# Attention and gated long convolution in one kernel: q, k, v on 96 partitions, q transposed by DMA, o in 64x64 tiles, and a new time order

## The chip, the cores and the metric

The kernel runs on one core of one Trainium2 chip. The metric is the device time of one execution in microseconds (us), the median of several runs. The core's engines work side by side, each on its own list of instructions: TensorE (PE) multiplies matrices, VectorE (DVE), ScalarE (ACT) and GpSimd (POOL) work element by element, and SyncE (SP) issues DMAs. POOL and ACT issue DMAs as well. An engine that waits for a semaphore holds everything behind it on its own list.

## The reference: what is computed

The inputs are q, k, v as float32 arrays of 8 batches x 8 heads x 576 times x 64, g_norm (64), w_proj (512x1536), filter_fft (576x512) and w_out (512x512).

```
kv  = einsum('bhsd,bhse->bhde', k, v)              # per head, 64x64
out = einsum('bhsd,bhde->bhse', q, kv)             # linear attention
x   = out / sqrt(mean(out*out, -1) + 1e-6) * g_norm # then heads side by side: B, 576, 512
x1, x2, x3 = split(x @ w_proj, 3)
x2c = irfft(rfft(x2, axis=1) * rfft(filter_fft, axis=0), n=576)
result = (x1 * x2c * x3) @ w_out                   # B, 576, 512
```

The sum over time in kv doesn't depend on the order of the 576 times. Everything after it depends on that order only through the tables of the transform, the rows of the filter and the rows that the result is written to.

## The kernel before, in words

**Time order.** The kernel keeps the 576 times in an order of its own: three thirds of 192 times for a transform of radix 3, and within a third three blocks of 64 times that lie 3 apart. On 128 partitions a block of 64 is half a tile. The same order is built into the tables of sines and cosines (`tvi`, L120), into the filter's rows `fa` and `fc` (L139 to L148), and into the rows of the result (`o_rows`, L475).

**Loads.** All loads go through POOL's DMA queue and turn float32 into bfloat16 on the way. k and v of a batch come as four DMAs (`load_kv`, L67): the main part puts four times of a head on each of 128 partitions (runs of 1 KB in memory), and a tail of 64 times goes to `kt`, `vt`, whose upper half stays zero. q comes as two DMAs (`load_q`, L77) in the kernel's time order, runs of 768 B. There are two buffers of each, so batch b+2 is loaded during batch b into the buffers that batch b used.

**Attention of batch b+1** is done during batch b. `kv` (L215) makes the 64x64 products of the heads in 40 matmuls (L223) and ACT copies the result into the block diagonal `kvblk` (L234). `qtr` (L236) transposes q on TensorE in 36 small transposes into PSUM (L247), and ACT copies that to `qT` in two copies (L256, DVE in batch 0). `att_o(b, j)` (L258), for each of the four pairs of heads j, multiplies `qT` with `kvblk` in two matmuls (L265); ACT takes the square `sq` (L266) and the copy `osb` (L271). `att_r` (L273) sums the squares over a head with a matmul, and ACT makes `rstd` (L281). DVE multiplies (`att_x`, L289) and folds the thirds (`fold`, L291 to L307).

**Convolution of batch b.** `proj2` (L363) projects x to x2 in the frequency order's folded form; `fft(b, g)` (L388) transforms in three groups g = 1, 0, 2 and multiplies with the filter (L408, L409, L417), the adds that make Y being on POOL for group 1, and in batch 0 for group 0 too (L411). `proj13(b, dc)` (L419) makes a quarter of x1 and x3 in 16 matmuls (L428); ACT copies x1 (L432) and DVE multiplies to `g13` (L434). `inv` (L436) transforms back from Y (L454, L456), `outp` (L480) multiplies with w_out (L488, L492), ACT copies to `ot` (L496; three buffers), and SP writes the rows (L499, L501). The output of batch b-1 is made during batch b. In the last batch `last` (L521) ends with five pieces `out1` (L503), whose DMAs (L519) go out on SP and in part on POOL or ACT.

**PSUM** is four tiles `ps` that every product takes in turn (L54), so a matmul may have to wait until ACT or DVE has emptied a tile.

**Order.** The program text gives the order as priorities; a scheduler then places the instructions of each engine, with some held in program order by `keep_in_program_order`. The loop that sets the order in each batch is this:

```
for dc in range(NDC) if b else ():
    if dc < 3:
        add = fft(b, (1, 0, 2)[dc]) or add
    if nxt:
        att_o(b + 1, dc)
    proj13(b, dc)
    if dc == 2:
        add()
    if nxt:
        att_r(b + 1, dc)
        ...
```

Ahead of it in each batch stand `proj2(b)`, `kv(b + 1)`, `qtr(b + 1)` and the loads of batch b+2. `outp` stands after dc = 1 and after the loop, and `inv` ends the batch.

Of the kernel before, what the change touches and what calls it, by code (L numbers as in the profile page):

```python
# [15 lines left out]
P = 128  # L16
# [4 lines left out]
def kernel(  # L21
# [40 lines left out]
    NR = S // 64  # L62
    kvm = [[consts.tile([P, H, 4, D], BF16, name="%sm%d" % (n, i)) for n in "kv"] for i in range(2)]
    kvt = [[consts.tile([P, H, D], BF16, name="%st%d" % (n, i)) for n in "kv"] for i in range(2)]
    qb = [consts.tile([P, 4, NR * D], BF16, name="qb%d" % i) for i in range(2)]

    def load_kv(b, *parts):  # L67
        for h0, h1 in parts:
            for i, src in enumerate((k, v)):
                nc.gpsimd.dma_start(  # L70
                    out=kvm[b % 2][i][:, h0:h1].rearrange("p h c d -> p h (c d)"),
                    in_=bass.AP(tensor=src.tensor, offset=src.offset + (b * H + h0) * S * D,
                                ap=[[4 * D, P], [S * D, h1 - h0], [1, 4 * D]]))
                if h0 == 0:
                    nc.gpsimd.dma_start(out=kvt[b % 2][i][:TAIL], in_=src[b, :, 4 * P:S, :].transpose([1, 0, 2]))

    def load_q(b):  # L77
        for g in range(2):
            nc.gpsimd.dma_start(  # L79
                out=qb[b % 2][64 * g:64 * g + 64].rearrange("p h (m x) -> p (h m) x", m=3),  # L80
                in_=bass.AP(tensor=q.tensor, offset=q.offset + (b * H + 4 * g) * S * D,
                            ap=[[3 * D, 64], [SB * D, 12], [1, 3 * D]]))


    kvblk = [consts.tile([P, 4, P], BF16, name="kvblk%d" % i) for i in range(2)]
    for i in range(2):
        for t in kvt[i]:
            nc.vector.memset(t[TAIL:P], 0.0)
        nc.vector.memset(kvblk[i], 0.0)
# [15 lines left out]
    load_q(0)  # L105
# [14 lines left out]
    nc.gpsimd.iota(tvi, pattern=[[2 * SB, 2], [2, 3], [6, 64]], base=1, channel_multiplier=0)  # L120
# [17 lines left out]
    fidx = consts.tile([P, 3], I32)  # L138
    for a, r0, n, base in ((0, 0, 64, 0), (0, 64, 64, 1), (1, 0, 64, 2), (1, 64, 64, SB), (2, 0, 32, SB + 1)):  # L139
        nc.gpsimd.iota(fidx[r0:r0 + n, a:a + 1], pattern=[[0, 1]], base=S - 1 - base, channel_multiplier=-3)  # L140
    for r0, n, a, na, base, step in ((0, 64, 0, 2, 0, 2), (64, 64, 0, 2, 1, SB - 1), (0, 32, 2, 1, SB + 1, 1)):
        nc.gpsimd.dma_start(out=fa[r0:r0 + n, a:a + na], in_=bass.AP(
            tensor=moe_filter_fft.tensor, offset=moe_filter_fft.offset + base * DM,
            ap=[[3 * DM, n], [step * DM, na], [1, DM]]))
    for a in range(3):
        n = P if a < 2 else 32
        nc.gpsimd.indirect_dma_start(out=fc[:n, a], out_offset=None, in_=moe_filter_fft,
                                     in_offset=bass.IndirectOffsetOnAxis(ap=fidx[:n, a:a + 1], axis=0))  # L148

    load_q(1)  # L150
# [64 lines left out]
    def kv(b, j0=0, j1=NDC):  # L215
        (km, vm), (kt, vt) = kvm[b % 2], kvt[b % 2]
        kvp = ps_tile("ps_kv")
        for j in range(j0, j1):
            for c in range(NSC):
                for hp in range(2):  # L220
                    h = 2 * j + hp
                    kk, vv = (km[:, h, c], vm[:, h, c]) if c < 4 else (kt[:, h], vt[:, h])
                    mm = nc.tensor.matmul(kvp[64 * hp:64 * hp + 64, 0, j * D:(j + 1) * D], kk, vv,  # L223
                                          start=(c == 0), stop=(c == NSC - 1))
                    if b == 1:
                        tc.keep_in_program_order(mm)
        for h in range(2):
            r = slice(64 * h, 64 * h + 64)
            o_ = kvblk[b % 2][r, j0:j1, r]
# [5 lines left out]

    def qtr(b, jjs=(0, 1)):  # L236

        s = st.setdefault(b, {})
        if jjs[0] == 0:
            s['qTc'] = work.tile([P, NDC, NR, 64], BF16, name="qT", tag="qT")  # L240
            s['qT'] = s['qTc'].rearrange("p j c t -> p j (c t)")
        qT = s['qTc']
        for jj in jjs:
            tp = psp.tile([P, 2, 1024], BF16, name="ps_qT", tag="ps").rearrange("p a b -> p (a b)")
            for c in range(NR):
                for hp in range(2):
                    mm = nc.tensor.transpose(tp[64 * hp:64 * hp + 64, c * P:(c + 1) * P],  # L247
                                             qb[b % 2][:, 2 * jj + hp, c * D:(c + 1) * D], ident)
                    if b == 1:
                        tc.keep_in_program_order(mm)  # L250
            o_ = qT[:, 2 * jj:2 * jj + 2].rearrange("p g c t -> p c g t")
            i_ = tp[:, 0:NR * P].rearrange("p (c g t) -> p c g t", c=NR, g=2)
# [5 lines left out]
    def att_o(b, j):  # L258
        s = st[b]
        if j == 0:  # L260
# [291 lines left out]
    for b in range(B):  # L552
# [13 lines left out]
        elif nxt:  # L566
            kv(b + 1)
            qtr(b + 1)
# [75 lines left out]
```

## Time and profile before

| | |
|---|---|
| device time, median of 3 runs | 239.54 us (239.22 to 240.31) |
| span of the profiled execution | 238.0 us |
| PE busy | 213.9 us (90%) |
| DVE busy | 197.2 us (83%) |
| ACT busy | 156.0 us (66%) |
| POOL busy | 72.1 us (30%) |
| POOL's DMA queue | 40,256 packets, 17.70 MB |
| SP's and ACT's DMA queue | 5,122 packets, 8.92 MB |

The span runs from the first to the last recorded event of one profiled execution; some 1.5 us of the device time lie around it (239.54 less 238.0). The profile gives the busy time of each engine, the chain of work that ended last, followed back from the last instruction, groups of instructions by their source line, and a timeline of each engine in which a bracket tells how long the engine was idle before an instruction and what released it. A busy share is an average over the whole span and tells little of any one stage: the first 50 us are loads and tables, then six batches of nearly the same shape follow, then an end of its own.

### The profile page before, as it was taken

What the parts mean: (1) busy time and instruction counts of PE and PEld (TensorE: products, weight loads), DVE (VectorE), ACT (ScalarE), POOL (GpSimd) and SP (SyncE); (2) the same over time, 40 slices, a digit from 0 to 9 for tenths busy, and PEclk for the clock granted to TensorE, in tenths of its full rate; (3) what the DMA queues carried; (4) which work ended last, traced back from release to release, by engine and by line L of the source; (5) the groups of instructions that cost most, each with busy time, mean ns of one, the idle gap of its engine ahead of it and who ended that gap; (6) DMA issues with size and microseconds to landing.
All of it is one profiled execution on the core that took longest, in us unless ns stands there. A gap on an engine that the chain in (4) does not pass through costs nothing.

```text
span 238.0 us, 4900 instructions
## 1 busy us (share of the span) xinstructions
PE 213.9 (90%) x1960; PEld 128.5 (54%) x1960; DVE 197.2 (83%) x376; ACT 156.0 (66%) x237; POOL 72.1 (30%) x96
## 2 busy tenths in 40 slices
PE   4978897685999999999999999999999999999960
PEld 1434354363576657665667566656675666566420
DVE  7759574799989798979797989797979897999860
ACT  2754528971887689776977697769776977642520
POOL 7963971490280029000910091002100210021010
PEclk9999999999999999999999999999999999999997
DMA  6999999999099129914992399250033003400346
GB/s 63 163 190 230 227 192 197 191 192 108 3 155 198 45 77 158 203 38 126 121 193 74 91 118 188 83 135 0 4 88 88 3 0 91 132 0 3 94 122 181
DMA packets 45559, 27.17 MB, mean 114 GB/s; under 512 B 22274, under 2 KB 40706, under 8 KB 45538
## 3 DMA queue, kind: packets, MB, share of 16 engines
q0 software_dynamic: 40256, 17.70, 58.8%
q1 hardware_dynamic: 5122, 8.92, 13.9%
q8 instruction: 15, 0.25, 0.4%
q10 hardware_dynamic: 160, 0.26, 0.4%
q14 instruction: 6, 0.05, 0.1%
HBM read 33.69 MB, written 9.44 MB: 181 GB/s over the span
## 4 chain that ended last, share of the span: by engine, by line
PE 61%; ACT 15%; DVE 8%; DMA 8%; issue 3%; POOL 3%; POOLq 0%; DVEq 0%; ACTq 0%
PE ps_x L428 20%; PE ps_out L488 10%; ACT qT L256 6%; PE ps_x L378 6%; DMA fc<-in_moe_filter_fft_dram,fidx 5%; DMA km<-in_k_dram 3%; PE ps_x L384 2%; PE ps_x L369 2%; PE ps_o L265 2%; PE ps_r L280 2%; ACT kvblk L234 2%; PE ps_invo L454 2%; PE ps_inve L454 2%; PE ps_kv L223 2%; ACT osb L271 2%
## 5 line engine op out<-in xcount | busy, mean ns | idle before, releaser
L428 PE MATMUL ps_x<-x,wp 128*128 128x288 bf16 x512 | 68.0, 286 | 1.5 <-DVE FX L210 1.5
L428 PEld LDWEIGHTS <-wp 128*128 128x128 bf16 x512 | 49.8, 98 | 15.3 <-issue 2.6
L411 POOL TENSOR_TENSOR Y<-tpw 128x1024 bf16<-128x1024 f32 (+1 forms) x9 | 21.2, 2354 | 68.7 <-PE ps_x L428 43.2
L434 DVE TENSOR_TENSOR g<-ps_x,x 128x576 bf16<-128x576 f32 x32 | 24.1, 754 | 9.8 <-ACT x L432 9.7
L432 ACT CAST x<-ps_x 128x576 bf16<-128x576 f32 x32 | 20.7, 646 | 10.4 <-PE ps_x L428 10.4
L70 POOL DMA_DIRECT2D km<-in_k_dram x9 | 7.8, 871 | 64.4 <-PE ps_kv L223 64.4
L488 PE MATMUL ps_out<-wo,yg 128*128 128x512 bf16 x112 | 26.6, 379 | 0.0
L281 ACT ACTIVATE rstd<-ps_r,bias_eps 128x576 bf16<-128x576 f32 x32 | 23.3, 742 | 4.8 <-PE ps_r L280 4.8
L496 ACT COPY ot<-ps_out 128x1024 f32<-128x1024 f32 (+1 forms) x17 | 15.9, 937 | 13.8 <-PE ps_out L488 13.8
L266 ACT ACTIVATE sq<-ps_o 128x576 bf16<-128x576 f32 x32 | 20.7, 653 | 5.6 <-PE ps_o L265 5.6
L408 DVE TENSOR_TENSOR tpw<-ps_X,HH 128x1024 f32<-128x1024 f32 (+1 forms) x16 | 19.5, 1221 | 5.1 <-PE ps_X L406 4.4
L271 ACT ACTIVATE osb<-ps_o,g_col 128x576 bf16<-128x576 f32 x28 | 20.8, 742 | 0.0
L409 DVE TENSOR_TENSOR tpw<-ps_X,HH 128x1024 f32<-128x1024 f32 (+1 forms) x16 | 19.4, 1213 | 0.0
L458 ACT COPY os<-ps_invo 128x576 f32<-128x576 f32 x14 | 9.0, 640 | 12.9 <-PE ps_x L372 5.1
L488 PEld LDWEIGHTS <-yg 128*128 128x128 bf16 x112 | 10.8, 98 | 10.4
L265 PE MATMUL ps_o<-qT,kvblk 128*128 128x288 bf16 x64 | 12.8, 287 | 3.7 <-ACT kvblk L234 2.1
L378 PE MATMUL ps_x<-wp,ab 128*128 128x512 bf16 x64 | 15.5, 381 | 0.6 <-DVE ab L307 0.3
L256 ACT COPY qT<-ps_qT 128x1152 bf16<-128x1152 bf16 x14 | 15.1, 1122 | 0.1
L280 PE MATMUL ps_r<-sq,ind 128*128 128x288 bf16 x64 | 13.1, 286 | 1.6 <-ACT osb L271 0.8
L79 POOL DMA_DIRECT2D qb<-in_q_dram x16 | 12.5, 784 | 6.3 <-DMA wp<-in_moe_w_proj_dram 3.1
L535 PE MATMUL ps_w<-kvblk,ind 128*128 128x512 bf16 x33 | 11.1, 486 | 3.7 <-DVE ind L103 3.4
L374 ACT CAST x<-ps_x 128x1024 bf16<-128x1024 f32 x8 | 8.1, 1016 | 8.4 <-PE ps_x L372 8.4
(177 smaller groups left out, 414.8 us busy)
## 6 DMA issues: line engine op xcount, KB each, us to landing
out_dram<-ot SPq DMA_DIRECT2D x28, 256.0 KB, 3.3
qb<-in_q_dram POOLq DMA_DIRECT2D x16, 288.0 KB, 7.1
km<-in_k_dram POOLq DMA_DIRECT2D x7, 512.0 KB, 6.2
vm<-in_v_dram POOLq DMA_DIRECT2D x7, 512.0 KB, 8.4
wp<-in_moe_w_proj_dram POOLq DMA_DIRECT2D x3, 512.0 KB, 10.6
out_dram<-ot SPq DMA_DIRECT2D x10, 128.0 KB, 3.2
km<-in_k_dram POOLq DMA_DIRECT2D x2, 256.0 KB, 5.6
kt<-in_k_dram POOLq DMA_DIRECT2D x8, 64.0 KB, 5.7
```

The costliest lines, as they stand in the source:

```text
L256: nc.scalar.copy(out=o_, in_=i_)
L266: nc.scalar.activation(out=s['sq'][:, j].rearrange("p (a b) -> p a b", a=2), in_=op[:, :, 0:TH], func=AF.Square)
L271: nc.scalar.activation(out=o_, in_=op[:, :, 0:TH], func=AF.Copy, scale=g_col)
L281: nc.scalar.activation(out=s['rstd'][:, j].rearrange("p (a b) -> p a b", a=2), in_=r2[:, :, 0:TH], func=AF.Abs_reciprocal_sqrt, scale=1.0 ...
L378: nc.tensor.matmul(pp[:, h], ab[:, j, h * SB:h * SB + P], wp[:, j, DM:2 * DM], start=(j == 0), stop=(j == NDC - 1))
L408: nc.vector.tensor_mul(out=t_[:n, 0], in0=xp[:n], in1=HH[:n, g, 1:3])
L409: nc.vector.tensor_mul(out=t_[:n, 1], in0=xp[:n], in1=HH[:n, g, 0:2])
L411: nc.gpsimd.tensor_add(out=Y[:n, 2 * g:2 * g + 2], in0=t_[:n, :, 0], in1=t_[:n, :, 1])
L428: nc.tensor.matmul(pp[:, h, 0:TH], w_, x[:, j, h * TH:(h + 1) * TH], start=(j == 0), stop=(j == NDC - 1))
L432: nc.scalar.copy(out=x1, in_=pp[:, :, 0:TH])
L434: nc.vector.tensor_mul(out=st[b]['g13'][:, dc].rearrange("p (a b) -> p a b", a=2), in0=pp[:, :, 0:TH], in1=x1)
L488: nc.tensor.matmul(pp[:, cc], yg[:, dc, c * P:(c + 1) * P], wo[:, dc], start=(dc == 0), stop=(dc == NDC - 1))
```

## The change

q, k and v of a batch each come with one DMA onto 96 partitions, six following times of a head on each (runs of 1.5 KB), with no tail. `kv` has six products per head instead of five. Its result goes to `kvblk` of another layout, by three copies instead of two. q is transposed on TensorE for batches 0 and 1 only, in 24 transposes of 96x128; from batch 2 on SP issues one transposing DMA per batch (`qtr_dma`) from the loaded tile to `qT`, which has two buffers now. `att_o` does two pairs of heads at once, each half of the rows in 64x64 products into their own quarters of TensorE. The views `by_time` and `by_row` put the times in order as ACT writes `osb` and `rstd`. The time order becomes 18 blocks of 32 times that lie 6 apart (`t_of`); the tables, the filter rows (`fa` now also by gathering DMA, with 18 index instructions instead of 5) and the output rows follow it, so that each piece of the output goes out in four DMAs instead of two. The diff gives the program's text; the scheduler's order follows from it.

```diff
+    NB = S // 32
+    def t_of(blk):
+        return SB * (blk // 6) + blk % 6 // 3 + 2 * (blk % 3)
+    TR = S // 6
+    kvq = {n: [consts.tile([TR, H, 6, D], BF16, name="%sb%d" % (n, i)) for i in range(2)] for n in "kvq"}
+    def load(n, b, h0=0, h1=H):
+        src = dict(k=k, v=v, q=q)[n]
+        nc.gpsimd.dma_start(
+            out=kvq[n][b % 2][:, h0:h1].rearrange("p h c d -> p h (c d)"),
+            in_=bass.AP(tensor=src.tensor, offset=src.offset + (b * H + h0) * S * D,
+                        ap=[[6 * D, TR], [S * D, h1 - h0], [1, 6 * D]]))
...
+            load("k", b, h0, h1)
+            load("v", b, h0, h1)
+    kvblk = [consts.tile([P, 2, 4, D], BF16, name="kvblk%d" % i) for i in range(2)]
...
-    nc.gpsimd.iota(tvi, pattern=[[2 * SB, 2], [2, 3], [6, 64]], base=1, channel_multiplier=0)
+    nc.gpsimd.iota(tvi, pattern=[[2 * SB, 2], [2, 2], [4, 3], [12, 32]], base=1, channel_multiplier=0)
...
+    fidx = consts.tile([P, 2, 3], I32)
+    for i in range(9):
+        for w, (first, step) in enumerate(((t_of(i), 6), (S - 1 - t_of(i), -6))):
+            nc.gpsimd.iota(fidx[32 * (i % 4):32 * (i % 4) + 32, w, i // 4:i // 4 + 1], pattern=[[0, 1]],
+                           base=first, channel_multiplier=step)
+    for w, dst in enumerate((fa, fc)):
+        for a in range(3):
+            n = P if a < 2 else 32
+            nc.gpsimd.indirect_dma_start(out=dst[:n, a], out_offset=None, in_=moe_filter_fft,
+                                         in_offset=bass.IndirectOffsetOnAxis(ap=fidx[:n, w, a:a + 1], axis=0))
...
+    load("q", 1)
...
-            for c in range(NSC):
+            for c in range(6):
                 for hp in range(2):
-                    h = 2 * j + hp
-                    kk, vv = (km[:, h, c], vm[:, h, c]) if c < 4 else (kt[:, h], vt[:, h])
-                    mm = nc.tensor.matmul(kvp[64 * hp:64 * hp + 64, 0, j * D:(j + 1) * D], kk, vv,
-                                          start=(c == 0), stop=(c == NSC - 1))
+                    mm = nc.tensor.matmul(kvp[64 * hp:64 * hp + 64, 0, j * D:(j + 1) * D], kk[:, 2 * j + hp, c],
+                                          vv[:, 2 * j + hp, c], start=(c == 0), stop=(c == 5))
...
+        lo, hi = slice(0, 64), slice(64, P)
+        for r, w, slot in ((slice(0, P), slice(0, P), 0), (lo, hi, 1), (hi, lo, 1)):
+            o_ = kvblk[b % 2][w, slot, j0:j1]
             i_ = kvp[r, 0, j0 * D:j1 * D].rearrange("p (j e) -> p j e", e=D)
             if b == 0 and j0 == 0:
                 nc.vector.tensor_copy(out=o_, in_=i_)
             else:
                 nc.scalar.copy(out=o_, in_=i_)
...
+    def new_qT(b):
+        st.setdefault(b, {})['qT'] = work.tile([P, H * 3, TR], BF16, name="qT", tag="qT", bufs=2)
+        return st[b]['qT']
+    def qtr_dma(b):
+        nc.sync.dma_start_transpose(out=new_qT(b), in_=kvq["q"][b % 2].rearrange("p h c d -> p (h c d)"))
...
+        qT = new_qT(b) if jjs[0] == 0 else st[b]['qT']
...
+            tp = psp.tile([P, 2, 1024], BF16, name="ps_qT", tag="ps")
+            for i in range(12):
+                h, c2 = 4 * jj + i // 3, i % 3
+                mm = nc.tensor.transpose(tp[:, i // 6, (i % 6) * TR:(i % 6 + 1) * TR],
+                                         kvq["q"][b % 2][:, h, 2 * c2:2 * c2 + 2].rearrange("p c d -> p (c d)"),
+                                         ident[:TR, :TR])
+                if b == 1:
...
+    def by_time(t, j):
+        return t[:, j].rearrange("p (m a r) -> p a m r", m=3, a=2)
+    def by_row(t):
+        return t[:, :, 0:TH].rearrange("p a (m r) -> p a m r", m=3)
+    def att_o(b, *js):
...
+        ops = [ps_tile("ps_o") for _ in js]
+        for j, op in zip(js, ops):
+            for r in range(2):
+                for hp in range(2):
+                    nc.tensor.matmul(op[64 * hp:64 * hp + 64, r, 0:TH], kvblk[b % 2][64 * r:64 * r + 64, r ^ hp, j],
+                                     s['qT'][64 * r:64 * r + 64, 6 * j + 3 * hp:6 * j + 3 * hp + 3].rearrange("p c (m t) -> p m c t", m=3),
+                                     start=True, stop=True)
+        for j, op in zip(js, ops):
+            nc.scalar.activation(out=s['sq'][:, j].rearrange("p (a b) -> p a b", a=2), in_=op[:, :, 0:TH], func=AF.Square)
+            if b == 0:
+                nc.vector.tensor_scalar_mul(out=by_time(s['o'], j), in0=by_row(op), scalar1=g_col)
+            else:
+                nc.scalar.activation(out=by_time(s['o'], j), in_=by_row(op), func=AF.Copy, scale=g_col)
...
-        nc.scalar.activation(out=s['rstd'][:, j].rearrange("p (a b) -> p a b", a=2), in_=r2[:, :, 0:TH],
+        nc.scalar.activation(out=by_time(s['rstd'], j), in_=by_row(r2),
...
-        t0 = [SB * (x // 3) + x % 3 for x in blks]
+        t0 = [t_of(x) for x in blks]
         two = [[(t0[1] - t0[0]) * DM, 2]] if len(t0) == 2 else []
-        return bass.AP(tensor=out.tensor, offset=out.offset + (b * S + t0[0]) * DM, ap=[[3 * DM, 64]] + two + [[1, DM]])
+        return bass.AP(tensor=out.tensor, offset=out.offset + (b * S + t0[0]) * DM, ap=[[6 * DM, 32]] + two + [[1, DM]])
...
+            for i in range(4):
+                r = slice(32 * i, 32 * i + 32)
                 if n == 2:
-                    nc.sync.dma_start(out=o_rows(b, 2 * c0 + i, 2 * c0 + 2 + i), in_=ot[64 * i:64 * i + 64])
+                    nc.sync.dma_start(out=o_rows(b, 4 * c0 + i, 4 * c0 + 4 + i), in_=ot[r])
                 else:
-                    nc.sync.dma_start(out=o_rows(b - 1 + i, NR - 1), in_=ot[64 * i:64 * i + 64, 0])
+                    nc.sync.dma_start(out=o_rows(b - 1 + i // 2, NB - 2 + i % 2), in_=ot[r, 0])
...
+        for i in range(4):
+            bb, blk = (b, 4 * c + i) if c < 4 else (b - 1 + i // 2, NB - 2 + i % 2)
+            (q1 if i >= 2 else nc.sync).dma_start(out=o_rows(bb, blk), in_=ot[32 * i:32 * i + 32, 0])
...
             kv(b + 1)
-            qtr(b + 1)
         if b + 2 < B:
             load_kv(b + 2, (0, 8))
-            load_q(b + 2)
+            load("q", b + 2)
+            qtr_dma(b + 2)
...
-            if nxt:
-                att_o(b + 1, dc)
+            if nxt and dc % 2 == 0:
+                att_o(b + 1, dc, dc + 1)
```

`load_kv` is a call for k and one for v. In batch 0's attention `att_o(1, 0)`, `att_o(1, 1)` become one call ahead of `fft(0, 1)`, and `att_o(1, 2)`, `att_o(1, 3)` one call ahead of `proj13(0, 2)`.

More of the change, by code (lines that the diff above doesn't have):

```diff
@@ L256, in qtr @@
                 nc.scalar.copy(out=o_, in_=i_)
[L258 removed]
+    def by_time(t, j):
[3 more added lines that the diff above has]
+    def att_o(b, *js):
         s = st[b]
[L260 removed]
+        if js[0] == 0:
             s['sq'] = work.tile([P, NDC, S], BF16, name="sq", tag="sq")
             s['o'] = work.tile([P, NDC, S], BF16, name="osb", tag="osb")
[L263 to L271 removed]
+        ops = [ps_tile("ps_o") for _ in js]
[11 more added lines that the diff above has]
+                nc.scalar.activation(out=by_time(s['o'], j), in_=by_row(op), func=AF.Copy, scale=g_col)
     def att_r(b, j):
@@ L535, in warm @@
             tc.keep_in_program_order(nc.tensor.matmul(
-                pp[:, 0], ind, kvblk[1].rearrange("p a b -> p (a b)"), start=True, stop=True))
+                pp[:, 0], ind, kvblk[1].rearrange("p a b c -> p (a b c)"), start=True, stop=True))
     warm(14)
```

78 lines of the change are left out of this document (8 added, 70 removed).

## The prediction

> **What bounds the kernel now.** I read the page first: the slices, then the chain that ended last. A digit of a slice is the busy share in tenths.
>
> ```profile
> PE   4978897685999999999999999999999999999960
> ...
> ACT  2754528971887689776977697769776977642520
> ...
> PE 61%; ACT 15%; DVE 8%; DMA 8%; issue 3%; POOL 3%; POOLq 0%; DVEq 0%; ACTq 0%
> PE ps_x L428 20%; PE ps_out L488 10%; ACT qT L256 6%; PE ps_x L378 6%; DMA fc<-in_moe_filter_fft_dram,fidx 5%; DMA km<-in_k_dram 3%; PE ps_x L384 2%; PE ps_x L369 2%; PE ps_o L265 2%; PE ps_r L280 2%; ACT kvblk L234 2%; PE ps_invo L454 2%; PE ps_inve L454 2%; PE ps_kv L223 2%; ACT osb L271 2%
> ```
>
> PE is at 9 in most slices after the first quarter, yet it holds only 61% of the chain; ACT holds 15%, of which L256, the copies of transposed q, has 6%. So in each batch there is a stretch where PE waits for ACT. The chain in order of time shows it; the columns are start, length, what. This is the batch that starts at 107.15, one of six nearly alike (starts 57.16, 82.36, 107.15, 130.93, 155.9, 179.6, 204.5).
>
> ```profile
> 111.55 0.66 PE ps_kv L223 x40
> 112.23 0.36 ACT kvblk L234
> 112.61 0.37 ACT kvblk L234
> 113.00 2.14 ACT qT L256 x2
> 115.14 0.56 ACT sq L266
> 115.69 0.62 ACT osb L271
> 116.32 0.54 ACT x L432
> 116.90 0.38 PE ps_X L399
> ```
>
> From `kv`'s end (112.21) to group 0 of `fft` (116.90) lie 4.69 us, all of them ACT's: two copies of kvblk, two of qT, then sq, osb, x1; PE has work in that time (L404 at 113.12, L428 from 114.41), but none that shortens it. The 36 transposes on PE (L247) are not in the chain; they lie beside ACT's work. After 116.90 the chain is PE's without a gap to the end of the batch, with 7.40 us from one output product (120.16) to the next (127.56).
>
> The third view is POOL's timeline around batch 0's end and PE's there (start, length, engine, line; the bracket is the idle time before and its releaser).
>
> ```profile
> 47.08 2.36 POOL L411 TENSOR_TENSOR Y<-tpw 128x1024 bf16<-128x1024 f32 x1 [2.92 <-DVE tpw L409]
> ...
> 50.10 2.36 POOL L411 TENSOR_TENSOR Y<-tpw 97x1024 bf16<-97x1024 f32 x1
> 52.40 1.50 POOL L79 DMA_DIRECT2D qb<-in_q_dram  x2
> ```
>
> ```profile
> 55.49 0.26 PE L454 MATMUL ps_invo<-IV,Y 128*128 128x192 bf16 x1 [2.17 <-DVE Y L417]
> ```
>
> POOL makes Y for batch 0 in two adds of 2.36 us, the last done at 52.46, and only then issues the next q load. PE's `inv(0)` starts at 55.49 and ends at 57.16.
>
> The fourth is the timeline of the last 9 us; SPq and ACTq are the issuing of DMAs.
>
> ```profile
> 230.48 3.49 SPq L519 DMA_DIRECT2D out_dram<-ot  x4
> ...
> 230.88 0.55 ACTq L519 DMA_DIRECT2D out_dram<-ot  x1
> ...
> 231.70 0.50 ACTq L519 DMA_DIRECT2D out_dram<-ot__3338  x1
> 234.07 0.55 SPq L519 DMA_DIRECT2D out_dram<-ot__3338  x1
> ```
>
> SP issues six DMAs from 229.89 on, about 0.55 to 0.87 us each, the last ending at 234.62 and landing at 236.52; ACT's two, issued at 230.88 and 231.70, land at 234.76 and 235.23. The span ends at 238.0, and 1.5 us lie around it (median 239.54).
>
> **Batches 1 to 6.** PE loses 36 transposes (1.11 us in one batch by the windows), and gains eight matmuls of `kv` at 16 ns (0.65 for 40): 0.13. `att_o` takes 4 x 0.25 = 1.0 now; four 64x64 products in their own quarters would take half of it, if they run side by side as L405 and L406 do (both start at 113.66, on two halves of the rows). PE's work falls by 1.11 + 0.5 - 0.13 = about 1.4 us per batch. It is not on the path where it falls, so I replace ACT's chain.
>
> Stretch one, kv's end to fft's group 0: three kvblk copies at 0.37 (1.11), the first `att_o` (0.13), then sq and osb of two pairs of heads, one behind the other, since both are one call now: 2 x (0.56 + 0.62) = 2.36, then x1 0.54; with 0.1 for hand-offs 4.25. That is 0.45 less than 4.69, and the second `att_o` that stood on the path at 117.71 (0.24) is inside it: -0.7.
>
> Stretch two, output to output: 1.73 for the output product, then ACT's copy ot (1.01), then again sq, osb, sq, osb (2.36) ahead of x1 (0.65). Four PSUM tiles are held by ot, by fft and by the two `att_o`, so the sixteen matmuls of the next `proj13` get a tile only after x1: 1.73 + 1.01 + 2.36 + 0.65 + 0.15 hand-off + 1.96 + 0.24 = 8.1 against 7.40: +0.7. Together **0 per batch**. Bounds: -1.4 x 6 = -8.4 if ACT does not hold PE up; and, if the quarters run one after another, sixteen matmuls of 0.125 instead of eight, +1.0, and sq 0.4 later: +1.4 x 6 = +8.4. I take 0, as the waits worked out from ACT's rows are the nearest. By windows PE is busy 24.4 us of a 24-us batch, so what ends last is not settled by shares.
>
> On the quarters, the Trainium skill ("TensorEngine Tiling (Array Packing)", Key Properties) has it that different tiles execute independently and in parallel; the trace shows that for two halves of rows, none of four quarters. By that rule the +8.4 falls away.
>
> **The transposing DMA in batch 0.** In the built order of the changed program POOL's list has, ahead of both Y adds of batch 0, the load of q(4), which waits for the transpose of q(2): they share a buffer. So Y(0), `inv(0)` and all behind them on PE wait for that DMA. q(2) landed at 49.25; four tails of 0.47 us are gone ahead of it on the full queue, so 47.4. For the transpose itself (0.59 MB, in 144 tiles of 16 rows x 128 columns: 2,304 pieces of 256 B read, 18,432 runs of 32 B written) there is no row. Low end: the 256 KB output DMA, 3.3 us from issue to landing, and for q itself as much when the queue is full: 3.5. High ends: runs at 8.6 ns, the 4-byte packets of g_col, 18,432 x 8.6 / 16 + 2 = 12; at 32 ns, the 128-byte packets, 39. Between: 2,304 pieces at 56 ns, the mean packet of POOL's queue (58.8% of 16 x 238 us over 40,256), over 16 engines, 8.1 + about 1 to start: **9**, the row nearest in size. Then: landing 56.5, q(4)'s issue 0.76 to 57.3, two adds 4.72 to 62.0, inv 1.67 to 63.7 instead of 57.16: +6.5. Batch 1 then waited for DVE (0.95 and 0.17 at L369 and L378): from L369 to L378 it took 2.88, against 1.42 in the batch of 107.31. I count 1.3 of that as over by then: **+5.2**. With 3.5 it is 0, with 12 +8, with 20 +16.
>
> Two pages of the Trainium skill differ here. "DMA: Bandwidth & Descriptors" (Latency and other measured facts) gives DMA_TRANSPOSE an effective 261 GB/s, an estimate of 2.3 us here and a term of 0. The table named at rival C gives some 24. The trace before has no transposing DMA, so neither is borne out by it.
>
> In later batches the same wait has over 20 us of slack (q(3) is in at 58.93, needed by batch 2's `att_o` near 87), and costs nothing until the transpose takes that long. SP's output DMAs behind a waiting transpose have three ot buffers, over 10 us, as cover.
>
> **Startup.** The load of q(1), 3.3 us, now stands ahead of the filter's rows in POOL's queue; q(0), k(0), v(0) are some 1.0 shorter without tails and the rows of fa by gathering are about as long as now. The filter comes 1.9 later, covered by the wait of Y(0) above; without that cover it would cost at most 1.9. Thirteen more index instructions on POOL lie beside the weights' loads. kt's and vt's memsets go, off the path.
>
> **The tail.** SP has twelve DMAs of 32 rows from 229.9 on, ACT four. In the built order SP's second DMA of piece c0 reuses a semaphore of the ACT DMAs of the last piece c3, so it waits for their landing: issue 231.70 + 3.2 (landing of the 128 KB ones) = 234.9; then that and eight more at 0.55: 234.9 + 0.55 + 4.4 = 239.85 against 234.62: **+5.2**; +3.5 with the landing at 2.4 and some issues overlapping, +7 at 0.75 each. In the steady batches the doubled output DMAs on SP (4 x 0.55 to 0.87 per piece, a piece every 7 us or more) are covered.
>
> **Sum**: 238.0 + 5.2 + 0 + 5.2 = 248.4; with 1.5 around it 249.9, **250**.
>
> **Rivals.**
>
> B, the transpose is as quick as a load: 238.0 + 0 + 5.2 + 1.5 = 244.7. For: its bytes are those of a q load (3.3 us). Against: the 32-byte runs; by packet records 128 B take 32 ns and 2 KB only 120, so small ones are dear. Chance 0.20. The Trainium skill's 261 GB/s, named above, would be this case.
>
> C, the small runs pay each: 20 us or more, Y(0) waits to 68: 238.0 + 16 + 5.2 + 1.5 = 261, and more if longer. For: the record prices above. Against: priced by the 256-byte pieces read it is 9. Chance 0.13. The Trainium skill ("VectorE: DVE Perf Modes", The three transpose paths) has 1.309 us for 128x128; 18 such one by one would be an estimate of 24 us.
>
> D, faster: ACT's copies of qT (2.14 per batch) were what held PE, and the double `att_o` does not replace them, because PE finds other work while sq and osb run. Then PE's 1.4 is kept, 8.4 in six batches; with the batch-0 term at 0 and the tail at +3.5: 238.0 - 8.4 + 3.5 + 1.5 = 234.6. It decides once the saving per batch passes (batch 0 + tail) / 6, 0.6 at the low ends and 1.7 at mine. For: ACT is busy 66% only and L256 is 6% of the chain. Against: the four-tile sum above. Chance 0.10.
>
> E, quarters one after another: 238.0 + 8.4 + 5.2 + 5.2 + 1.5 = 258.3. Chance 0.07.
>
> The forecast, A, with its neighbours (transpose 7 to 11, tail +3.5 to +7: 245.5 to 254): 0.50. That the change would not do what it says is excluded: the built program has six transposing DMAs and no PE transposes after batch 1.
>
> **Range.** 241.5 to 262 holds A, most of B and E, and half of C; it leaves out D (0.10), B's low edge (0.03) and C's upper half (0.06). A measurement here tells about 0.5%, 1.2 us, from no change. Faster than 238.3: D without its upper edge, 0.09; within: 0.04; slower: 0.87.
>
> **What will show it.** Right: in the after profile POOL's q(4) issue idles for the DMA qT, then two adds, and `inv(0)` ends near 63; the transpose takes about 9 us from issue to landing; batches keep a period near 24.4 with ACT's sq, osb, sq, osb on the chain; SP's last issue ends near 240. Wrong: a transpose of 2 to 4 or over 14 us; batch periods near 23 (D) or 26 (E); SP's last DMA landing near 238.

## The result, and the profile after

The changed kernel takes 253.19 us (median of four runs, 252.73 to 253.95) against 239.93 for the kernel before beside it: a ratio of 1.054 (95% interval 1.048 to 1.061). It is slower by 13 us, with 250.0 forecast and 241.5 to 262 as the range. The profiled execution took 253.22 with a span of 251.4, so 1.8 us lie around it.

The page of the changed kernel, slices and chain:

```profile
PE   6658988790599999999999999999999999999850
...
ACT  2745238980157757775778486857675966632420
...
PE 54%; ACT 18%; DMA 11%; POOL 7%; issue 5%; DVE 1%; SPq 0%; POOLq 0%; ACTq 0%; DVEq 0%
PE ps_x L434 17%; PE ps_out L494 9%; DMA qT<-qb 5%; PE ps_x L384 5%; DMA fc<-in_moe_filter_fft_dram,fidx 5%; ACT osb L277 5%; ACT kvblk L227 3%; ACT sq L273 3%; PE ps_x L375 3%; ACT ot L502 2%; PE ps_x L390 2%; PE ps_invo L460 2%; PE ps_inve L460 2%; PE ps_kv L216 2%; PE ps_r L286 2%
```

PE's busy time is the same as before (213.7 us against 213.9), but only in sum: from batch 1's start to batch 7's PE is busy for 140.2 us where it was 144.6, and up to batch 1's start for 48.1 where it was 43.8, with a mean granted clock of 0.86 instead of 1.00 there. ACT has risen from 15% to 18% of the chain, and `DMA qT<-qb`, the transposing DMA, is in it with 5%. The copies of transposed q (6% before) are gone. The slices, of 6.3 us each here, show the place of the largest loss: from 57 to 63 us PE is at 0 and from 63 to 69 us at 5. Before, the lowest there was one slice at 5, and from 60 us on PE was at 9.

The starts of the batches, read from PE's timeline (the first matmul of `proj2`), split the 13.4 us of span into three places. The same table holds for the experiments below; all spans are of profiled executions.

| kernel | batch 1 starts | two steady periods | from batch 7's start to the end | span |
|---|---|---|---|---|
| before | 57.16 | 24.84, 23.78 | 33.6 | 238.0 |
| after | 69.33 | 24.84, 23.78 | 35.8 | 251.4 |
| q3 | 65.16 | 24.84, 23.76 | 35.8 | 247.0 |
| q3one | 63.16 | 24.05, 22.98 | 35.8 | 240.2 |
| pe_tr | 63.48 | 26.49, 25.42 | 35.7 | 256.3 |
| split | 56.98 | 24.85, 23.79 | 36.0 | 240.2 |
| kvlate | 65.47 | 24.83, 23.78 | 35.8 | 248.5 |
| inorder | 57.23 | 24.84, 23.77 | 35.8 | 240.3 |
| bef_q1 | 57.89 | 24.85, 23.78 | 33.6 | 238.2 |
| best | 57.97 | 24.05, 22.98 | 35.1 | 234.5 |
| best_again | 59.53 | 24.05, 22.98 | 35.0 | 236.8 |
| best2 | 62.91 | 24.04, 22.99 | 34.6 | 239.9 |
| q3warm | 69.76 | 24.83, 23.78 | 35.8 | 251.9 |
| q3warm_again | 66.11 | 24.84, 23.78 | 35.9 | 247.9 |

Batch 1 starts 12.2 us late; 0.9 of it is back within batch 1 (24.24 instead of 25.15), which leaves 11.3. The steady batches have their old length to 0.01 us. The end is 2.2 us longer. 11.3 + 0 + 2.2 is the 13.4.

**Batch 0.** POOL's timeline (the loads at 44.73 and 45.49 are those of k(3) and v(3)), with the load of q(4) (61.10) ahead of the two Y adds:

```profile
44.73 0.77 POOL L73 DMA_DIRECT2D kb<-in_k_dram  x1 [3.04 <-PE ps_kv L216]
45.49 0.77 POOL L73 DMA_DIRECT2D vb<-in_v_dram  x1
61.10 0.77 POOL L73 DMA_DIRECT2D qb<-in_q_dram  x1 [14.84 <-DMA qT<-qb]
61.93 4.63 POOL L417 TENSOR_TENSOR Y<-tpw 128x1024 bf16<-128x1024 f32 x2
```

PE's timeline there, `inv(0)`:

```profile
64.33 0.34 PE L460 MATMUL ps_invo<-IV,Y 128*128 128x192 bf16 x1 [7.67 <-POOL Y L417]
...
66.62 0.26 PE L462 MATMUL ps_invo<-IV,Y 97*128 97x96 bf16 x1 [1.63 <-POOL Y L417]
```

POOL waits 14.84 us for the transpose, adds Y, and PE, idle for 7.67 and 1.63 us on the way, gets through `inv(0)` at 69.33. The transpose was issued at 47.30 and landed at 60.55, 13.2 us.

**A steady batch.** The chain in order of time, from `kv` to the second output product:

```profile
122.81 0.78 PE ps_kv L216 x48
...
123.61 0.37 ACT kvblk L227
...
124.00 0.36 ACT kvblk L227
...
124.38 0.38 ACT kvblk L227
...
125.16 0.65 ACT sq L273
125.81 0.64 ACT osb L277
...
127.88 0.22 PE ps_X L405
...
130.74 0.21 PE ps_out L494
...
132.50 0.96 ACT ot L502
...
133.95 0.75 ACT osb L277
134.70 0.54 ACT sq L273
135.24 0.63 ACT osb L277
135.87 0.54 ACT x L438
...
136.45 2.12 PE ps_x L434 x16
...
138.82 0.21 PE ps_out L494
```

The second stretch of before, which the prediction gives in words, from the same view of the kernel before:

```profile
120.16 1.73 PE ps_out L488 x8
...
122.56 0.35 PE ps_o L265 x2
122.91 1.96 PE ps_x L428 x16
...
125.11 0.24 PE ps_o L265 x2
125.36 1.96 PE ps_x L428 x16
...
127.56 1.73 PE ps_out L488 x8
```

Against the lines of before: three copies of kvblk follow `kv`; sq and osb of one pair of heads follow, and then eight matmuls of PE (L434, 126.50) that wait for osb. The other pair's sq and osb (126.33 to 127.61 on ACT) and x1 lie beside those and are not on the chain. In the second stretch ot, sq, osb, sq, osb, x lie one behind the other on ACT (the chain counts the first sq, at 133.41, as a wait before osb), and PE's next sixteen matmuls (136.45) wait for x; before, that stretch was PE's alone. From `kv`'s end (123.58) to group 0 of `fft` (127.88) are 4.30 us, where 4.69 were; from output to output (130.74 to 138.82) 8.08, where 7.40 were.

**The end.** Issues on SP and ACT:

```profile
241.13 0.79 SPq L526 DMA_DIRECT2D out_dram<-ot__3196  x2
...
242.02 5.96 SPq L526 DMA_DIRECT2D out_dram<-ot  x8
...
242.94 0.87 ACTq L526 DMA_DIRECT2D out_dram<-ot__3240  x2
...
248.09 0.84 SPq L526 DMA_DIRECT2D out_dram<-ot__3240  x2
```

SP's second DMA of piece c0 (the first of the eight went out at 242.02) went out at 244.69, when ACT's DMA of 242.94 had landed (244.67); the rest followed it, the last issue ending at 248.93 and landing at 250.22.

### The profile page after: what moved, and what is told of

The parts are those of the page before. It is cut to its first block, busy times and chain, and to the rows that moved or that the text cites. A ratio compares the mean times of both kernels' runs of the same rounds, so it can differ in the third digit from the quotient of the medians.

```text
span 251.4 us, 4699 instructions
## 1 busy us (share of the span) xinstructions
PE 213.7 (85%) x1820; PEld 123.3 (49%) x1848; DVE 193.2 (77%) x373; ACT 146.6 (58%) x233; POOL 57.9 (23%) x87
## 4 chain that ended last, share of the span: by engine, by line
PE 54%; ACT 18%; DMA 11%; POOL 7%; issue 5%; DVE 1%; SPq 0%; POOLq 0%; ACTq 0%; DVEq 0%
PE ps_x L434 17%; PE ps_out L494 9%; DMA qT<-qb 5%; PE ps_x L384 5%; DMA fc<-in_moe_filter_fft_dram,fidx 5%; ACT osb L277 5%; ACT kvblk L227 3%; ACT sq L273 3%; PE ps_x L375 3%; ACT ot L502 2%; PE ps_x L390 2%; PE ps_invo L460 2%; PE ps_inve L460 2%; PE ps_kv L216 2%; PE ps_r L286 2%
## 5 line engine op out<-in xcount | busy, mean ns | idle before, releaser
L434 PE MATMUL ps_x<-x,wp 128*128 128x288 bf16 x512 | 70.1, 286 | 4.1 <-ACT ot L502 1.1
L434 PEld LDWEIGHTS <-wp 128*128 128x128 bf16 x512 | 49.1, 97 | 24.2 <-issue 11.1
L494 PE MATMUL ps_out<-wo,yg 128*128 128x512 bf16 x99 | 25.8, 379 | 0.7
L466 DVE TENSOR_TENSOR u<-ps_inve,os 128x576 bf16<-128x576 f32 x14 | 10.5, 752 | 10.4 <-ACT os L464 10.4
L73 POOL DMA_DIRECT2D qb<-in_q_dram x8 | 6.4, 803 | 45.9 <-DMA qT<-qb 38.9
L73 POOL DMA_DIRECT2D kb<-in_k_dram x9 | 6.9, 767 | 42.7 <-PE ps_kv L216 35.6
L269 PE MATMUL ps_o<-qT,kvblk 64*64 64x288 bf16 x128 | 11.9, 304 | 5.6 <-remote 2.8
L460 PEld LDWEIGHTS <-Y 128*128 128x128 bf16 x128 | 10.0, 103 | 10.5 <-POOL Y L417 8.0
L460 PE MATMUL ps_invo<-IV,Y 128*128 128x192 bf16 x56 | 8.6, 262 | 7.7 <-POOL Y L417 7.7
L286 PE MATMUL ps_r<-sq,ind 128*128 128x288 bf16 x64 | 13.7, 301 | 0.6 <-issue 0.3
## 6 DMA issues: line engine op xcount, KB each, us to landing
vb<-in_v_dram POOLq DMA_DIRECT2D x7, 576.0 KB, 10.2
```

The costliest lines, as they stand in the source:

```text
L434: nc.tensor.matmul(pp[:, h, 0:TH], w_, x[:, j, h * TH:(h + 1) * TH], start=(j == 0), stop=(j == NDC - 1))
L460: nc.tensor.matmul(p_[h][:, i, 0:SB], Y[:, 2 * g + h, cs], IV[:, 2 * g + h, 0:SB], start=(g == 1), stop=(g == 2))
L494: nc.tensor.matmul(pp[:, cc], yg[:, dc, c * P:(c + 1) * P], wo[:, dc], start=(dc == 0), stop=(dc == NDC - 1))
```

## The experiments

Each edit is to the changed kernel unless the heading says otherwise. Before, beside them, had medians of 240.6 to 242.4.

### q3: three buffers for q

```diff
-    kvq = {n: [consts.tile([TR, H, 6, D], ...) for i in range(2)] for n in "kvq"}
+    NQ = dict(k=2, v=2, q=3)
+    kvq = {n: [consts.tile([TR, H, 6, D], ...) for i in range(NQ[n])] for n in "kvq"}
...
+ kvq["q"][b % 3]   # wherever q's buffer is read; loads use b % NQ[n]
```

> The changed kernel with a third buffer for q, so that the load of q(4) no longer waits for the transposing DMA of q(2). Theory 1 (that wait holds Y of batch 0, inv(0) and all behind it on PE): batch 1 starts near 58 instead of 69.5, and the time falls by about 11 us, from 253.2 to 242 (241 to 243.5), although the transpose itself still takes over 10 us beside the loads. Rival (batch 0 is late by the later filter rows, or by the transpose crowding loads that batch 0 and 1 need): the time stays above 247 and batch 1 starts after 63.

Measured: 249.1 us (ratio to before 1.036, 1.028 to 1.044). The Y adds no longer wait for the transpose (they start at 53.43), and the time falls, but by 4 us only: batch 1 starts at 65.16, as the rival had it. So the wait was the last of two late chains; 8 us of another lie beneath it. The figure of theory 1 falls; its wait is shown.

### q3one: one pair of heads at a time

```diff
-            if nxt and dc % 2 == 0:
-                att_o(b + 1, dc, dc + 1)
+            if nxt:
+                att_o(b + 1, dc)
```

with three q buffers as in q3.

> As with the third q buffer, and o for one pair of heads at a time in batches 1 to 6, at the places where the kernel before had it; the 64x64 tiles and the transposing DMA stay. Theory 2 (the two sq and osb in a row on ACT take back what PE saves): the period of a batch falls by 0.7 to 1.2 us, and the time is 5 to 7 below the kernel with three q buffers, 235 to 237. Rival (the saving is lost elsewhere, in the third kvblk copy, in changes of tile mode, or DVE is the next bound): within 1.5 us of it, 240.5 to 243.5.

Measured: 243.7 us, 5.4 below q3. The time itself, 235 to 237, was missed, since it was counted from theory 1's figure for q3. Every steady batch is 0.79 us shorter (24.05 and 22.98), 4.7 in six, and theory 2 holds: the two sq and osb in a row did take back what PE saved. (In the spans q3one is 6.8 us shorter than q3; the other 2.0 are an earlier start of batch 1, which this edit doesn't touch.) The chain of this kernel has the four quarter products in it:

```profile
116.75 0.31 PE ps_o L270 x3
117.06 2.07 PE ps_x L435 x16
...
120.02 0.25 PE ps_o L270 x4
120.27 2.07 PE ps_x L435 x16
```

Four 64x64 products (the second row has all four; in the first a record is missing) take 0.25 us from their start to the next instruction on PE, as the two of 128x128 did before (0.24). They run together (all four start within 0.01 us, at 119.95 to 119.96), but the hoped-for 0.12 per pair did not come. In the changed kernel, where eight stand in a row, the second four start 0.15 us after the first (124.80 and 124.95); so much of the 0.25 falls between the four and the 128x128 product behind them. What it is spent on no run shows. PE's busy time over two batches is 46.17 against 48.12, 0.98 less for each, which is the transposes less `kv`'s eight more matmuls.

### pe_tr: TensorE transposes in every batch

```diff
             kv(b + 1)
+            qtr(b + 1)
...
-            qtr_dma(b + 2)
```

> The changed kernel with q transposed on TensorE in every batch (24 transposes and two ACT copies), no transposing DMA. Theory 1: with no such DMA nothing holds Y of batch 0, batch 1 starts near 58, -11. Theory 2: ACT's two qT copies, about 2 us, come back into the stretch between kv and group 0 of fft, ahead of the two sq and osb: +1.5 to +2.1 for each of six batches, +9 to +13. Together 251 to 255. Rival to 2 (PE or DVE is the bound there, and the copies lie beside it): 242 to 245.

Measured: 257.6 us, above the 251 to 255 expected. Each batch is 1.65 us longer, as theory 2 had it. The chain shows why:

```profile
121.17 0.78 PE ps_kv L216 x48
...
121.97 0.37 ACT kvblk L227
...
123.13 2.15 ACT qT L252 x2
...
127.89 0.22 PE ps_X L405
```

The two copies of qT, 2.15 us on ACT, stand on the path again, and `kv`'s end to group 0 is now 5.94 us. Batch 1 starts at 63.48, 5.5 us later than theory 1 said, with no transposing DMA at all: the second late chain again, and the reason for the miss. What the DMA saves in a steady batch is thus 1.65 us, nearly all of it ACT's time; the double `att_o` and the third kvblk copy take as much.

### split: the kernel before with its output DMAs cut in two

```diff
-  nc.sync.dma_start(out=o_rows(b, 2 * c0 + i, 2 * c0 + 2 + i), in_=ot[64 * i:64 * i + 64])
+  for r in range(2):
+      nc.sync.dma_start(out=o_rows(b, 2 * c0 + i, 2 * c0 + 2 + i, r=r),
+                        in_=ot[64 * i + 32 * r:64 * i + 32 * r + 32])
```

and the same in `outp`'s last piece and in `out1`.

> The kernel before with each output DMA of 64 rows cut into two of 32, and nothing else. Theory 3 (SP's issues, and its wait for ACT's last DMAs, set the end): the stretch after the last batch grows by 2 to 2.5 us and the batches keep their length, so the time is 241.5 to 242.5. Rival (the end of the changed kernel is late by its clock or by the order of copies): 239 to 240.3. Second rival (the doubled issues also delay the batches through the ot buffers): above 244.

Measured: the median is 244.6 (242.1 to 245.5; ratio to before 1.017, 1.010 to 1.024), which lies in the second rival's range. The profiled execution was the fastest of the five, 242.1: its start and periods are as before, its end 36.0 instead of 33.6, +2.3. SP's issues:

```profile
230.64 5.99 SPq L522 DMA_DIRECT2D out_dram<-ot  x8
```

Eight issues take 5.99 us because one of them, as in the changed kernel, waits for ACT's DMAs to land. Theory 3 holds for the end in that execution, and its batches are not delayed. The other four took 2.4 to 3.4 us more, at a mean granted clock of 0.964 to 0.978 where it had 0.984; where they spent it no trace shows, so for them the second rival is not excluded.

### kvlate: k(3) and v(3) behind the Y adds

The loads of k and v for batch 3 and the two adds of batch 0 are held in the order of the text, so those loads are no longer under way beside the transpose of q(2).

```diff
+        if n in "kv" and b == 3:
+            tc.keep_in_program_order(dm)
...
+                if b == 0:
+                    tc.keep_in_program_order(ya)
```

> The changed kernel with the loads of k(3) and v(3) held behind the Y adds of batch 0; the wait of q(4) for the transpose of q(2) stays ahead of them. Theory 5 (the transpose takes 5 us by itself, as in the later batches, and 13 us in batch 0 because it shares the DMA engines with those loads): it takes 6 to 9 us here, Y is added 4 to 6 us sooner, and batch 1 starts near 65, where the late filter takes over; 248 to 250. Rival (the first transpose is slow by itself or by the second one behind it): it takes 12 us or more and the time stays at 252 to 254.

Measured: 249.8 us; batch 1 at 65.47. The DMA issues of this kernel (the last number is us from issue to landing) for the transpose of q(2), and then those of the changed kernel for a transpose in a later batch:

```profile
qT<-qb SPq DMA_TRANSPOSE x1, 6.1
```

```profile
qT<-qb SPq DMA_TRANSPOSE x1, 5.1
```

6.1 us without the loads, 13.2 with them, 5.1 in a quiet queue: theory 5 holds. The edit also parts the first transpose from the second, which the changed kernel issues at 54.31 beside it and this one at 54.87 behind its landing. But in the execution of q3warm below the second came behind the landing too (56.89, landing 56.58), and the first, with the load of q(4) issued 0.3 us behind it, still took 9.9 us; so a load is enough to slow it. With k(3) and v(3) beside it, it took 15.3 us in q3 and 16.1 in q3one.

### inorder: POOL's loads in the order of the text

```diff
+            tc.keep_in_program_order(...)   # the six gathers of the filter rows
...
+        if b:
+            tc.keep_in_program_order(dm)    # in load(), and in load_w for wo
```

> The changed kernel with POOL's loads and the gathers of the filter rows held in the order of the program text: the filter ahead of q(1), and every later load, q(4) among them, behind both Y adds of batch 0. Two q buffers as in the changed kernel. Theory 4 (with the wait for the transpose gone, 8 us remain in the kernel with three q buffers because the filter lands 2.8 us later, PE idles 4.9 us for it and then runs at a granted clock of 0.5): the filter lands near 28.5, the clock stays at 1.0 between 30 and 40, batch 1 starts at 57 to 59, and the time is 240.5 to 243, the tail's +2.2 over the kernel before. Rival (the start is late by the six gathers and eighteen index instructions themselves, or by the double o in batch 0): the filter still lands after 30 and batch 1 starts after 61, 245 to 249.

Measured: 242.1 us (ratio 1.004, 1.000 to 1.008). Batch 1 starts at 57.23, all 12.2 us of batch 0 are back, and what is left is the end. So the order on POOL's queue is the whole of batch 0's loss; q3 shows the part of Y behind q(4), 4 us. With the filter ahead of q(1), ff starts at 26.41, 1.6 us sooner than in the kernel before (28.05). The edit moves the other loads as well, so the filter's order by itself is not shown. One part of theory 4 is wrong: the clock does fall here, to 0.59 between 38 and 46, and the batch starts in time all the same.

### bef_q1: the kernel before with q(1) ahead of the filter

```diff
+    load_q(1)          # moved up, ahead of fa, and held in order
     fa = work.tile([P, 3, DM], FP32, name="fa", tag="tpw", bufs=2)
```

> The kernel before with one edit: the load of q for batch 1 stands ahead of the filter's rows on POOL's queue. Theory 4 (a filter that is late by one load makes PE idle long enough to lose its clock): the filter lands 3 us later, near 31, PE then runs at a clock near 0.5 for some us, and batch 1 starts 4 to 7 us later; 243.5 to 247. Rival (only the 3 us of the load itself, or less): 240 to 242.5 with the clock at 1.0.

Measured: 241.8 us, as before (1.000, 0.997 to 1.004), the rival's range. The filter lands at 30.95 instead of 28.27, and batch 1 starts only 0.7 us later; the granted clock falls once, to 0.5 from 56.1 to 59.5. DVE's timeline tells why; first q3, where batch 0 is late, then this kernel:

```profile
30.86 1.23 DVE L326 TENSOR_TENSOR ff<-fa,fc 128x1024 bf16<-128x1024 f32 x1 [6.21 <-DMA fc<-in_moe_filter_fft_dram,fidx]
32.00 0.55 DVE L201 COPY FW<-ps_ft 128x768 bf16<-128x768 bf16 x1
32.57 0.29 DVE L206 COPY FX<-ps_ft 64x256 bf16<-64x256 bf16 x1
```

```profile
25.05 0.56 DVE L207 COPY FW<-ps_ft 128x768 bf16<-128x768 bf16 x1 [0.36 <-PE ps_ft L206]
25.63 0.29 DVE L212 COPY FX<-ps_ft 64x256 bf16<-64x256 bf16 x1
30.85 3.55 DVE L321 TENSOR_TENSOR ff<-fa,fc 128x1024 bf16<-128x1024 f32 x4 [4.93 <-DMA fc<-in_moe_filter_fft_dram,fidx]
```

ff needs the filter; FW and FX are copies of tables out of PSUM, and PE's next product waits for that PSUM tile. In q3 ff stands ahead of them, as in the kernel before, so a late filter holds PE; here the scheduler has put them 5 us ahead of ff. So a late filter costs little by itself. It costs what stands behind ff. This was read from two traces; the changed kernel with FW ahead of ff was not run.

### q3warm and q3warm_again: PE kept busy while the filter is late

With three q buffers, and ahead of `proj13(0, 0)`:

```diff
+            for _ in range(80):
+                tc.keep_in_program_order(nc.tensor.transpose(hst["fts"][1][:, 1, 0], IV[:, 0, 0:P], ident))
```

In q3 PE idled 4.89 us for FX and then ran slowly (24 matmuls, 3.10 us in the kernel before):

```profile
32.92 5.70 PE L435 MATMUL ps_x<-x,wp 128*128 128x288 bf16 x24 [4.89 <-DVE FX L206]
```

> The kernel with three q buffers, and on PE, in the 5 us in which it waits for the filter, 80 more transposes of a table into an unused half of a PSUM tile; their result is never read. Theory 6 (the idle PE loses its granted clock: 0.5 from 31 to 38, 24 matmuls in 5.70 us instead of 3.10): the clock stays at 1.0 in that stretch, the 24 matmuls take 3.1, batch 1 starts 2.5 to 4 us sooner than at 65.2, and the time falls from 249.1 to 245 to 247. Rival (the clock falls for another reason, or what comes after waits for the loads anyway): the batch starts within 1 us of 65.2 and the time stays at 248 to 250.5.

Measured: 252.6 us (252.6 to 253.7), and nothing decided: ACT stood still for 3.3 us at 16.3 for a reason that the profile does not name, PE idled there instead, and the 80 transposes came on top. The kernel was run once more.

> Once more the kernel with three q buffers and 80 transposes on PE while it waits for the filter. The first time a stall of 3.3 us on ACT at 16.3 us, which the profile puts down to nothing on the core, moved PE's idle time ahead of those transposes, and they came on top. Theory 6: where that stall is absent, the transposes end near 32.5, the clock stays at 1.0 from 26 to 40, the 24 matmuls after them take 3.1 instead of 5.70 us, and batch 1 starts 2.5 to 4 us before 65.2: 245 to 247. If the stall is there again: 252 to 254 as before, and the clock's share stays a sum of durations. Rival: no stall, the clock falls all the same or the batch still starts near 65: 248 to 250.5.

Measured: 250.3 us, batch 1 at 66.11. The stall was absent. By stretches (PE's busy time first, the granted clock third from the end):

```profile
31.00:38.00 7.00, 6.44 (x58) 4.46 (x55) 5.49 (x8) 1.28 (x2) 4.20 (x8) 1.00 1.29 206
42.00:52.00 10.00, 9.11 (x77) 3.48 (x77) 4.12 (x6) 8.55 (x15) 0.32 (x1) 0.52 1.33 189
```

Between 31 and 38 the clock stayed at 1.00, where q3 had 0.53; but then it was 0.52 from 42 to 52, with PE busy for 9.1 of 10 us. The lead over q3 on PE is 1.9 us at q's transposes (40.06 against 41.97) and 0.5 at `att_o` (47.41 against 47.88): the slow stretch moved and took most of it. And the batch started no sooner for another reason, which POOL's and PE's timelines show:

```profile
55.84 0.77 POOL L74 DMA_DIRECT2D qb<-in_q_dram  x1 [13.52 <-DMA qT<-qb]
...
58.19 5.16 POOL L419 TENSOR_TENSOR Y<-tpw 128x1024 bf16<-128x1024 f32 x2
```

```profile
63.41 0.26 PE L464 MATMUL ps_invo<-IV,Y 97*128 97x96 bf16 x1 [2.39 <-POOL Y L419]
```

With the 80 transposes in the program the scheduler put the load of q(5), which waits for the transpose of q(2) with three buffers, and those of k(3) and v(3) ahead of the Y adds. So Y was added at 58.19 to 63.35, where q3 began at 53.43, and `inv(0)` waited for it: theory 1's wait is back. Whether a steady clock wins time is therefore not decided by these two runs, and what sets the slow stretch off is open.

### best, best2, best_again: a version that beats both

inorder and one pair of heads at a time, and in the end

```diff
-    for c, ev, q1 in (..., (1, act, nc.sync), ...):
+    for c, ev, q1 in (..., (1, act, nc.gpsimd), ...):
```

> POOL's loads in the order of the text, o for one pair of heads at a time in batches 1 to 6, and the second half of the last piece but two (c1) sent out by POOL instead of SP. By theories 2, 3 and 4: batch 1 starts near 58, six batches are 0.79 us shorter each (-4.8), the end is 1 us shorter than in the changed kernel (+1.2 over before): 235 to 238, faster than both. Rival: the batches before find the loads late, now that they wait behind the Y adds, and the time is 239 or more.

Measured: 236.8 us, ratio to before 0.981 (0.975 to 0.987). The terms came nearly as worked out: start 57.97, periods 24.05 and 22.98, end 35.1, which is 0.7 shorter than in the changed kernel where 1 was expected.

best2 adds, for the last piece, `(q1 if i >= 2 or c == 3 else nc.sync)`.

> The fastest version so far (236.8) with the four DMAs of the very last piece all on ACT, so that SP has eight in the last stretch instead of ten. Theory 3 (SP's row of issues sets the end): two issues of 0.45 us go, the last landing is 0.8 to 1 us sooner, the span after the last batch falls from 35.1 to about 34.2 us: 235.5 to 236.5. Rival (ACT's wait for its own last copy, or the landing, sets it): 236.5 to 237.5.

Measured: 241.7 us (238.7 to 242.3), though the end is shorter, 34.6. Its batch 1 starts at 62.9. In the profiled execution ACT stood idle for 5.2 us at 11.7, where best has 1.8; PE, whose products it waits for, ran at a granted clock of 0.51 from 9.0 to 12.4 (best: 1.00), so that `kv` began at 13.73 instead of 11.54, and everything after it was late. For the end theory 3 holds in part (-0.5 of the 0.9 expected); the total says nothing of it.

> The fastest version once more, in more rounds and beside the kernel before on another draw of the chip, since its sister with one edit in the last 4 us came out 5 us slower through its first 25 us. If the start is a draw (a stall in the first 25 us that comes and goes with the run, in either kernel): single times between 236 and 242, the six batches and the end as they were (24.05, 22.98; 35.1). Rival (the slower time belongs to the sister's edit): all times within 236 to 238.

Measured: 236.5 us (235.7 to 238.6), ratio 0.980 (0.974 to 0.986). The profiled execution was the slowest, 238.6, with a start at 59.53, the same periods and end. So the start does move between executions of one kernel, by 1.6 us in the two traces, and not as far as in best2; whether best2's edit has a part in its start stays open.

## Why the prediction was right, and where its sizes were off

**The steady batches** came out as worked out: 0 predicted, 0.01 measured, from two opposite changes of the sizes given (stretch one 4.25 predicted, 4.30 measured; stretch two 8.1 and 8.08). In stretch two the terms are the predicted ones. In stretch one the size is in part luck: behind the first sq and osb the chain runs through PE (eight matmuls and L286, 126.50 to 127.88), not through the second sq, osb and x1 as summed, which end at about the same time. That ACT's double `att_o` gives back the gain is shown by q3one (-0.79 a batch), and that the qT copies were the gain by pe_tr (+1.65). One part was wrong without harm: the 0.5 us that the quarter products were to save. The rule of the Trainium skill cited there ("TensorEngine Tiling (Array Packing)", Key Properties) agrees in that the four run together; with a 128x128 product behind them no time came of it. Rivals D (batches near 23 us) and E (near 26) did not occur. Two figures of the prediction are off without harm to its sum: 1.11 + 0.5 - 0.13 is 1.48 and not 1.4, and PE is busy for 24.1 us of a batch of 24.3 (48.12 of 48.63 in two), not 24.4 of 24.

**Batch 0** was the right mechanism with one term mis-sized: 5.2 predicted, 11.3 measured. q(2) landed as said (47.30; 47.4). The transpose took 13.2 us instead of 9, which is 4.2 of the 6.1 missing. The row chosen for it gave 8 us for 2,304 packets of 56 ns; in the changed kernel's later batches it takes 5.0 to 5.2 us, which is 34 ns a packet (so too in kvlate: 2,336 packets, 79% of 16 engines for 6.3 us), but k(3) and v(3) were under way on the same 16 engines, and kvlate takes those away and 7 us with them. The rest is 0.55 us from landing to the next issue, 1.0 for `inv(0)` at a granted clock of 0.50 between 60 and 70 (66.62 to 69.33, 2.7 us instead of 1.7), and 0.4 less given back.

Neither page of the Trainium skill named for the transpose gives its time. From issue to landing, 0.59 MB in 5.1 us are 116 GB/s, not the 261 GB/s of "DMA: Bandwidth & Descriptors"; while its packets flow without a pause, it comes above that (281 to 296 GB/s in kvlate's trace from 51.2 to 52.7), so as a rate for the bytes alone the figure is not contradicted. The 24 us that "VectorE: DVE Perf Modes" would make of it did not occur.

**The startup** was said to cost "at most 1.9" without the cover of Y's wait. That step fails: q3, kvlate and pe_tr have no such cover and start batch 1 6 to 8 us late. The filter comes 2.8 us later, where 1.9 was counted. That ff stands ahead of FW and FX on DVE, so that PE stops for it, was not looked for (before it cost PE 1.51 us, in q3 4.89), and in q3 24 matmuls at half the clock added 2.6. These are 5.4 of q3's 8.0 us; the rest is not split up here. It is hidden in the changed kernel's time, since the transpose is later still. Rival B (244.7 with a quick transpose) would therefore have been wrong: near 249, as q3 and kvlate show.

**The tail** was the right mechanism, SP's second DMA of c0 held until ACT's landed, with sizes too large: 5.2 predicted, 2.2 measured. ACT's DMA of 64 KB landed 1.73 us after issue, where 3.2 was taken from those of 128 KB, and SP's last nine issues follow each other by 0.48 us on average (244.69 to 248.50), where 0.55 was taken. So SP's second DMA of c0 went out 3.56 us after SP's first of the end (241.13 to 244.69) and not 5.0. By luck the two errors, +6.1 and -3.0, partly cancel; the sum's 250 is nearer to 253 than its terms are.

## What to carry to other kernels

A DMA that reads a load buffer makes that buffer's next load wait, and on a queue that works in order, everything behind that load waits too (14.84 us on POOL here): look where the scheduler has put it, and put work that others need ahead of it (inorder gave back 12 us by order alone). An edit elsewhere can move that order again, as q3warm's transposes on PE did, so look in each build. When copies leave an engine's chain, see what is placed in the gap: one large batch of work there can take the whole gain. Time a transfer with what else is on its queues, not alone.

## What the runs showed of the hardware

- In the changed kernel the transposing DMA of a 96x3072 bfloat16 tile held SP's list for 3.0 to 3.7 us in quiet batches and 6.9 in batch 0, and landed 5.0 to 5.2 us after issue, 13.2 us beside 1.2 MB of loads (15.3 and 16.1 in q3 and q3one).
- The granted clock of one busy core fell to 0.5 for 3.4, 6.8 or 10.2 us at a time, one to three times in the first 71 us of every profiled execution but before's: in q3 during a PE idle of 4.9 us, in inorder 2.2 us behind one of 1.1 us (36.11 to 37.21), and in before, which has the same 1.1 us (37.75 to 38.84), not at all. "TensorE: Matmul & The Clock Gate" of the Trainium skill (Part 1) gives an idle window of about 3.4 us for the fall and as much busy time for the return; 10 us at 0.52 with PE busy for 9.1 of them (q3warm_again) do not agree with the second.
- In the profiled executions of the changed kernel and of q3warm ACT stood idle for 2.8 and 3.3 us near 16 us, ahead of its copies of kvblk, where q3 has 0.4, with nothing on the core that the profile names as the releaser.
